# Three low halves of an expert's weights in an earlier turn, and a second-layer block inside three first-layer bodies

## The chip, the cores and the metric

The kernel runs on one core of one Trainium2 chip. The metric is the device time of one execution in microseconds. TensorE is PE below, VectorE is DVE, ScalarE is ACT, GpSimd is POOL, SyncE is SP.

## The reference

Attention over 8 batches and 8 heads, with keys and values averaged over 8 neighbours, gives 4608 tokens of 512 numbers. Tokens with a positive skip score go to one of 8 experts, the others stay as they are.

```python
x = attention(q, mean8(k), mean8(v))            # 4608 x 512
do_compute = x @ w_skip > 0
e_idx = argmax(x[do_compute] @ w_gate, axis=1)  # one expert of 8 per token
for e in range(8):                              # D = 512, F = 1024
    h = np.maximum(xc[e_idx == e] @ w1[e], 0.0)
    y[e_idx == e] = gate_w * (h @ w2[e])
out[do_compute] = xc + y
```

## The kernel before

**Attention and routing.** The attention runs in 36 turns, one for each tile of 128 tokens (`for t in range(NT)`, line 856). While it runs, finished tiles are routed in six groups (`GROUPS`, line 47): for every token of a group its place in a table, ordered by expert, is worked out, and POOL writes the tile's 128 rows into that table in DRAM by an indirect DMA (`write`, line 409; 33 of them). The order on every engine is the order in which the program is written. What POOL does beside its fixed work is handed to a small planner, `gps`, when the program is built: each piece has a first turn, a last turn and a cost, table writes stand in a list of their own, and in every turn `Paced.take` (line 667) puts out pieces of both lists until the turn's budget (`GPS`) is spent or no piece is ready.

**The early expert.** During attention the expert that leads the count so far is chosen, and its weights are loaded in eight chunks of 128 x 1024 (w1 in chunks 0 to 3, w2 in 4 to 7). Products run in fp32r; each weight is split into a high half, a rounded copy by ACT (`high`, line 602), and a low half, the weight less the high one (`low`, line 605), 512 columns at a time. Low halves up to chunk 6, half 0 go to POOL; `later_low` (line 696) gives them to the planner with the turns

```python
gps.add((now["t"] + 1, NT - 6, NT - 6, NT - 1, NT - 1)[max(cc - 2, 0)], wload(cc + 3) - 1 if cc < 3 else (NT - 3, NT - 1, NT + 9, NT + 9)[cc - 3],
        1.25, lambda: low(cc, i))
```

so that chunk 3 and 4 may go from turn 30 on and chunk 5 and 6 from turn 35 on (NT is 36). In the same stretch of POOL's queue stand: the copy of the last batch's values (`values_in`, line 250), read by PE when it makes the values of tile 31; the slots of 256 early tokens and two gathers of their rows (lines 515 and 517), which need ids that an SP transfer reads from the table (line 512); and the writes of the last 15 tiles that are written.

**Slots.** After the last turn, `slots` (from line 1006) works out, for every unit of work, which rows of the table it takes: a chain of some thirty small DVE operations from line 1020 to line 1061 (`coli`) and 1065 (`col`, s_col in the trace). PE needs s_col at line 1068. POOL then gathers the table's rows (line 1062), which needs `coli` and all table writes. A second chain, to line 1102 (s_both), gives the units' kinds, for which PE waits at line 1105; PE reads the gathered rows only at line 1114, behind that. Between these PE works off the first products of the early expert (`steps`).

**The expert loop.** From line 1147 on every engine has a program of its own with semaphores (`P` waits, `V` signals, line 1153). Tokens are worked on in units of up to three blocks ("places") of 128. For each unit PE runs the first layer (`first`, line 1366: 8 groups of 12 products) for a number of columns that depends on the unit's kind: `far_width` (line 1216) holds four bodies, for 256, 320, 288 and 384 columns, and branches to one of them; at its end a body branches to the common code behind all of them (line 1233). There a unit of a kind above TWO runs `second` for place 0 and for place 1 (24 products each), any other unit for place 1 at most; then come the transposes of the next unit and place 2. Within `second(0, True)` the products of k = 4 and k = 6 wait for the last three low halves of the first layer, which DVE writes. The branch hints (`marks`, `branch_hint`) tell the sequencer where a branch leads.

Of the kernel before, what the change touches and what calls it, by code (L numbers as in the profile page):

```python
# [40 lines left out]
NT = NTOK // 128  # L41
# [8 lines left out]
PICK, EARLY = 9, 18  # L50
PICKED = 15
LAST = 6
SCALE = 1.0 / (POOL * HD ** 0.5)
GMAX = max(GROUPS)
PLACED = GROUPS[-1]
# [102 lines left out]
def attention(tc, nc, q, k, vm, vr, cf, wg, w1, w2, whi, wlo, out, c, pay, offs, table, near, bufs, late, early, mb, fin, cfs):  # L158
    with ExitStack() as ctx:
# [38 lines left out]
        def keys(b, hh, gs=slice(0, 4)):  # L198

            r = halves[hh]  # L200
            nc.scalar.activation(kbd[b % 2][r, gs, hh * SP:(hh + 1) * SP], kps[b][r, gs], AF.Copy, scale=-SCALE)

# [116 lines left out]
        def values(t, pT, apart=False):  # L319
            if apart:  # L320
                os = [ps_s.tile([128, 512], F32, name="sc") for _ in range(2)]
            else:
                o = ps_o.tile([128, 2, 512], F32, name="o")
                os = [o[:, 0], o[:, 1]]
            for g in range(4):
                for hh, r, sl, b in blocks(t):
                    nc.tensor.matmul(os[hh][sl, g * VA:(g + 1) * VA], pT[r, g, sl], vb[b % 2][r, g, :], start=(g == 0), stop=False)
            for hh, r, sl, b in blocks(t):
                nc.tensor.matmul(os[hh][sl, 0:4 * VA], pT[r, 4, sl], vl4[b % 3][r].rearrange("p g c -> p (g c)"), start=False, stop=True)
            return [o_.unsqueeze(1) for o_ in os] if apart else [o]  # L330
# [193 lines left out]
        later, now = {}, {}  # L524
# [70 lines left out]
        def load_first(cc):  # L595
            nc.sync.dma_start(chunk_view(stage[:, room(cc)], cc), chunk_src(w1, w2, expert(0), cc))
# [4 lines left out]
        def high(cc, i):  # L601
            nc.scalar.activation(piece(whi, cc, i), stage[:, room(cc), i * 512:i * 512 + 512], AF.Copy)

        def low(cc, i, by=nc.gpsimd):
            return by.tensor_tensor(piece(wlo, cc, i), stage[:, room(cc), i * 512:i * 512 + 512],
                                    piece(whi, cc, i).bitcast(F32), ALU.subtract)
# [82 lines left out]
        act, dve, gps = Work(ACT), Work(DVE), Paced(GPS)  # L689

        def at(t, f):
            loads.setdefault(t, []).append(f)
# [3 lines left out]
        def later_low(cc, i):  # L696
            if cc * 2 + i > 12:
                rest.append(lambda v: low(cc, i, v))
            else:
                gps.add((now["t"] + 1, NT - 6, NT - 6, NT - 1, NT - 1)[max(cc - 2, 0)], wload(cc + 3) - 1 if cc < 3 else (NT - 3, NT - 1, NT + 9, NT + 9)[cc - 3],  # L700
                        1.25, lambda: low(cc, i))

        def adds(b, ready, last):
            first, small = sums(b)
            if b == 0:
                return first, small
            fs = [first[0], first[1], small[0], first[2], small[1], first[3], small[2], small[3]]
            for f, cost in zip(fs, (1.25, 1.25, 0.7, 1.25, 0.45, 0.7, 0.3, 0.7)):
                gps.add(ready, last, cost, f)

        def wload(cc):
            return PICKED + 9 * cc // 4 if cc < 8 else NT - 2
# [17 lines left out]
        for cc in range(8):  # L730
            at(wload(cc), lambda cc=cc: load_first(cc))
            for i in range(2 if cc < LAST else 0):
                act.add(wload(cc) + (3 if cc < 3 else 4), min(wload(cc) + 6, NT - 2), 0.55, lambda cc=cc, i=i: (high(cc, i), later_low(cc, i)))
# [42 lines left out]
        first, small = adds(0, 0, 0)  # L776
# [149 lines left out]
        os_[NT - 1] = values(NT - 1, pts.pop(NT - 1), True)  # L926
        for cc in range(LAST, 8):
            for i in range(2):
                high(cc, i)
                later_low(cc, i)  # L930
# [208 lines left out]
def experts(tc, nc, out, w1, w2, whi, wlo, slot, gate, nti, kinds_a, steps, lows, near, bufs, mb, ident, twice, psum, upper):  # L1139
# [7 lines left out]
    with tc.tile_critical(no_gpsimd_drain=True):  # L1147
# [4 lines left out]
        def P(e, n, by=1):  # L1152
            e.wait_ge(sem[n], by).then_inc(sem[n], -by)  # L1153
# [59 lines left out]
            with when(e, kind > TWO):  # L1213
                three(0, len(QUARTERS) - 1)

        def far_width(e, kind, go, marks):

            name = f"wide{nc.next_id()}"
            widths = [slice(128, 384)] + [slice(0, n) for n in QUARTERS]
            jumps, froms = [], []  # L1220
            for i, n in enumerate(FAR):
                froms.append(nc.cur_bb)
                jumps.append(e.br_cond(kind == TWO + n if n == NEAR else kind < TWO + n + 1, f"{name}_go{i}", f"{name}_not{i}"))
                jumps[i].branch_hint(marks[i])
                nc.switch_bb(f"{name}_not{i}")
            mark = e.mark_branch_hint_location()
            go(widths[-1])
            e.br(f"{name}_past").branch_hint(mark)
            for i, n in enumerate(FAR):
                with nc.body(f"{name}_go{i}", parent=froms[i], valid_engines=[e.engine]):  # L1230
                    mark = e.mark_branch_hint_location()
                    go(widths[n])
                    back = e.br(f"{name}_past")
                    if i + 1 < len(FAR):
                        back.branch_hint(mark)
            nc.switch_bb(f"{name}_past", parent=froms[0])
            return jumps
# [9 lines left out]
        with nc.Block(no_gpsimd_drain=True) as blk:  # L1247
# [89 lines left out]
            def _(t):  # L1337
                at, turn = parity(t, 1)
                
                def tx(u):  # L1340

                    o, after = at(), held[3]
                    t.reg_load(after, nti[0:1, bass.ds(u + 1, 1)])
                    three = t.snap(after, min_val=0, max_val=TWO + 4)
                    if LOOPED:
                        for jump, mark in zip(jumps, widths_ahead(t, after)):
                            jump.branch_hint(mark)
                    for i in range(3):
                        P(t, f"land{i}")
                    for unit, this in ((0, o < 1), (1, o > 0)):  # L1350
                        def place(i, n):
                            for k in range(4):
                                m = t.transpose(psD[i][:, k * 128:k * 128 + 128],
                                                ring[:, 3 * unit + i, k * 128:k * 128 + 128], ident)
                            m.then_inc(sem["pe"], n)

                        with t.If(this):
                            with t.If(three > TWO):
                                place(0, 1)
                                place(1, 1)  # L1360
                            with t.If(three < TWO + 1):
                                place(1, 2)
                            place(2, 1)
                    turn()
# [21 lines left out]
                def second(place, lo):  # L1386

                    i = place % 2
                    if place < 2:
                        P(t, f"psf{i}")  # L1390
                    sl, ps = slice(place * 128, place * 128 + 128), psF[i]
                    for k in range(8):
                        if lo and k in (4, 6):
                            for _ in range(k // 2 - 1):
                                P(t, "lo")
                        t.matmul(ps, hhi[:, k, sl], whi[1][:, k, :], start=(k == 0), stop=False)  # L1396
                        t.matmul(ps, hhi[:, k, sl], wlo[1][:, k, :], start=False, stop=False)  # L1397
                        last = t.matmul(ps, hlo[:, k, sl], whi[1][:, k, :], start=False, stop=(k == 7))  # L1398
                    last.then_inc(sem["l2"], 1)

                def unit(u, kind, ends, _, left):
                    jumps[:] = far_width(t, kind, first, marks)
                    with t.If(kind > TWO):
                        second(0, True)
                        second(1, False)
                    with t.If(kind < TWO + 1):
                        with t.If(kind > TWO - 1):
                            second(1, True)
                    with t.If(left > 1):
                        tx(u)  # L1410
                    with t.If(kind < TWO):
                        for _ in range(3):
                            P(t, "lo")
                    P(t, "psf0")
                    with t.If(ends < 2):
                        second(2, False)
                    with t.If(ends > 1):
                        second_short()
# [40 lines left out]
                marks, jumps = [], []  # L1459
                for n, (_, _, f) in enumerate(steps):  # L1460
                    if n == 5:
                        P(t, "lo")
                    i = int(not 4 <= n < 6)
# [4 lines left out]
                    if n == 3:  # L1468
                        marks = widths_ahead(t, held[1])
                    if n in BETWEEN:  # L1470
                        i = PLACES[BETWEEN.index(n)]
# [248 lines left out]
```

## Time and profile before

| | us |
|---|---|
| median of 3 runs (lowest to highest) | 488.16 (487.16 to 488.66) |
| the profiled execution, its own time | 485.97 |
| its span, first to last instruction | 484.2 |
| busy: PE / DVE / ACT / POOL | 460.1 / 286.7 / 233.8 / 204.2 |

The profile shows one execution. A timeline gives for each instruction its start and its length in us, and in brackets how long its engine was idle before it and which instruction ended that by the semaphores; where an engine waited for several things, the last one is named. "PEq" is PE's sequencer, which runs ahead of the array. Attention ends at about 140 us, the slot calculation runs from 144 to 162 us, the loop over experts from 163 to 479 us, with 11 whole units and one short one.

### The profile page before, as it was taken

Reading aid. Unit: us, or ns where it says so; the run is one execution under the profiler, and the core shown is the slowest. Engines: PE = TensorE matmul, PEld = TensorE weight load, DVE = VectorE, ACT = ScalarE, POOL = GpSimd, SP = SyncE. Lnnn points to the kernel's source line nnn. Section 1 sums busy time; section 2 is a strip of 40 time slices with the busy share of each in tenths; the row PEclk is TensorE's granted clock in tenths of the full one; section 3 lists DMA queues with packets and bytes.
Section 4 is the critical chain, followed back from the end, with each engine's and each line's share of the span. In section 5 each row is a group of like instructions: output and inputs, shape, how many; then the busy total and the mean of one; then the engine's idle time right before and its main releaser. Section 6 shows DMA issues by size and latency. Waiting matters only on the chain. (4 is left out here: it accounts for less than half of the span.)

```text
span 484.2 us, 12494 instructions
## 1 busy us (share of the span) xinstructions
PE 460.1 (95%) x4244; PEld 399.9 (83%) x4245; DVE 286.7 (59%) x659; ACT 233.8 (48%) x614; POOL 204.2 (42%) x271
## 2 busy tenths in 40 slices
PE   8999899999997998999999999999999999999993
PEld 7776677776886787898989899999898989899872
DVE  3677898988879435375765745323226442535663
ACT  4788799999861024173634534221215421424350
POOL 4588279987787331242304034232333222032020
PEclk9999999999998999999999999999999999999998
DMA  8999799966620283657572636111114542234110
GB/s 291 401 405 397 284 364 416 394 219 219 217 73 5 60 283 111 236 200 260 173 238 97 230 129 226 43 43 43 41 51 162 195 162 64 89 128 145 65 43 9
DMA packets 33214, 87.29 MB, mean 180 GB/s; under 512 B 6751, under 2 KB 7263, under 8 KB 31249
## 3 DMA queue, kind: packets, MB, share of 16 engines
q1 hardware_dynamic: 25728, 71.74, 41.0%
q0 software_dynamic: 7440, 14.99, 9.4%
q8 instruction: 24, 0.39, 0.4%
q14 instruction: 22, 0.17, 0.1%
HBM read 72.58 MB, written 20.19 MB: 192 GB/s over the span
## 5 line engine op out<-in xcount | busy, mean ns | idle before, releaser
L1374 PE MATMUL psl<-xhi,w1hi 128*128 128x256 f32 (+3 forms) x352 | 103.5, 294 | 0.3 <-PEq L1153 0.3
L1375 PE MATMUL psl<-xlo,w1hi 128*128 128x256 f32 (+3 forms) x352 | 103.4, 294 | 0.0
L1376 PE MATMUL psl<-xhi,w1lo 128*128 128x256 f32 (+3 forms) x352 | 103.4, 294 | 0.0
L1280 POOL DMA_INDIRECT out<-ring,slot x34 | 35.3, 1038 | 158.6 <-POOLq L1153 144.4
L1500 ACT ACTIVATE hhi<-psl 128x256 fp32r<-128x256 f32 (+3 forms) x88 | 36.2, 411 | 110.5 <-ACTq L1153 109.8
L1573 DVE SCALAR_TENSOR_TENSOR hlo<-psl,hhi 128x256 fp32r<-128x256 f32 (+1 forms) x88 | 38.0, 434 | 59.1 <-DVEq L1153 59.1
L300 ACT ACTIVATE e<-sc,mn 128x72 f32<-128x72 f32 x288 | 64.8, 341 | 9.1 <-DVE mn L295 8.8
L1374 PEld LDWEIGHTS psl<-xhi,w1hi 128*128 128x128 f32 x352 | 66.1, 188 | 1.1 <-issue 0.7
L1375 PEld LDWEIGHTS psl<-xlo,w1hi 128*128 128x128 f32 x352 | 66.1, 188 | 0.4
L1376 PEld LDWEIGHTS psl<-xhi,w1lo 128*128 128x128 f32 x352 | 66.1, 188 | 0.0
L1490 ACT ACTIVATE xhi<-psd 128x512 fp32r<-128x512 f32 x36 | 19.1, 599 | 75.9 <-ACTq L1153 75.9
L1275 POOL DMA_INDIRECT ring<-out,slot x36 | 40.4, 1122 | 19.5 <-issue 15.2
L409 POOL DMA_INDIRECT table<-pay,r_di x33 | 33.1, 1002 | 19.4 <-DVE p_two L434 9.1
L1396 PE MATMUL psf<-w2hi,hhi 128*128 128x512 f32 x96 | 38.2, 398 | 1.8 <-PEq L1153 1.8
L1550 DVE TENSOR_TENSOR w2lo<-stage,w2hi 128x1024 fp32r<-128x1024 f32 x28 | 34.2, 1224 | 9.5 <-DVEq L1153 9.5
L1397 PE MATMUL psf<-w2lo,hhi 128*128 128x512 f32 x96 | 37.5, 390 | 0.0
L1398 PE MATMUL psf<-w2hi,hlo 128*128 128x512 f32 x96 | 37.4, 390 | 0.0
L295 DVE TENSOR_REDUCE mn<-sc 128x4 f32<-128x288 f32 x72 | 30.7, 452 | 11.0 <-PE sc L287 7.2
L1550 DVE TENSOR_TENSOR w1lo<-stage,w1hi 128x1024 fp32r<-128x1024 f32 x28 | 32.4, 1220 | 3.4 <-DVEq L1153 3.3
L1397 PE MATMUL mb<-w2lo,hhi 128*128 128x512 f32 x88 | 34.3, 390 | 0.0
L1396 PE MATMUL mb<-w2hi,hhi 128*128 128x512 f32 x88 | 34.3, 390 | 0.0
L1398 PE MATMUL mb<-w2hi,hlo 128*128 128x512 f32 x88 | 34.3, 390 | 0.0
(293 smaller groups left out, 943.9 us busy)
## 6 DMA issues: line engine op xcount, KB each, us to landing
stage<-in_w SPq DMA_DIRECT2D x64, 512.0 KB, 4.7
out<-x SPq DMA_DIRECT2D x36, 256.0 KB, 5.8
stage<-in_k SPq DMA_DIRECT2D x7, 1152.0 KB, 9.0
qt<-in_q SPq DMA_DIRECT2D x9, 512.0 KB, 7.6
hlo<-in_vm SPq DMA_DIRECT2D x4, 1024.0 KB, 10.4
hhi<-in_vm SPq DMA_DIRECT2D x4, 1024.0 KB, 9.9
xhi<-in_q SPq DMA_DIRECT2D x4, 512.0 KB
xlo<-in_q SPq DMA_DIRECT2D x4, 512.0 KB, 9.6
```

What stands on the lines that cost most here:

```text
L300: nc.scalar.activation(e[:, g, hh * SP:(hh + 1) * SP], sc[:, h * SP:(h + 1) * SP], AF.Exp, bias=mn[:, 4 * i + h:4 * i + h + 1], scale=-1.0)
L1275: g.indirect_dma_start(ring[:, s % 6, 0:D], None, out, bass.IndirectOffsetOnAxis(ap=slot[:, s:s + 1], axis=0), bounds_check=NTOK - 1, oob_ ...
L1280: g.indirect_dma_start(out, bass.IndirectOffsetOnAxis(ap=offsets, axis=0), ring[:, s % 6, 0:D], None, bounds_check=NTOK - 1, oob_is_err=Fa ...
L1374: t.matmul(ps, whi[0][:, k, w], xhi[:, k, xs], start=(k == 0), stop=False)
L1375: t.matmul(ps, whi[0][:, k, w], xlo[:, k, xs], start=False, stop=False)
L1376: last = t.matmul(ps, wlo[0][:, k, w], xhi[:, k, xs], start=False, stop=(k == 3))
L1396: t.matmul(ps, hhi[:, k, sl], whi[1][:, k, :], start=(k == 0), stop=False)
L1397: t.matmul(ps, hhi[:, k, sl], wlo[1][:, k, :], start=False, stop=False)
L1398: last = t.matmul(ps, hlo[:, k, sl], whi[1][:, k, :], start=False, stop=(k == 7))
L1500: a.activation(hhi[:, f, xs], psL[f % 3][:, xs], AF.Relu).then_inc(sem["act"], 1)
L1550: v.tensor_tensor(chunk_of(wlo, c), chunk_view(stage[c], c), chunk_of(whi, c).bitcast(F32), ALU.subtract).then_inc(sem["wlo"], 1)
L1573: return v.scalar_tensor_tensor(out[:, f, :], psL[f % 3][:, xs], 0.0, hhi[:, f, xs].bitcast(F32), ALU.max, ALU.subtract)
```

## The change

A table `LOWS` gives the turns (first, last) of the low halves from chunk 3 on one by one. The two halves of chunk 3 and the first of chunk 4 get turn 29; the second of chunk 4 gets 31 to 33, those of chunk 5 get 32 to 34 and 33 to 35; the first of chunk 6 stays at 35 to 45. Lows of chunks 0 to 2 keep their turns.

`far_width` takes one more argument, code to be put behind a body; it is `second(0, True)`, and it is put into the three bodies that serve kinds above TWO (320, 288 and 384 columns), ahead of the branch to the common code, from which it is taken out.

```diff
+LOWS = (29, 29), (29, 29), (29, 29), (31, 33), (32, 34), (33, 35), (35, 45)
...
-                gps.add((now["t"] + 1, NT - 6, NT - 6, NT - 1, NT - 1)[max(cc - 2, 0)], ...
+                ready, last = LOWS[cc * 2 + i - 6] if cc > 2 else (now["t"] + 1, wload(cc + 3) - 1)
+                gps.add(ready, last,
                         1.25, lambda: low(cc, i))
...
-        def far_width(e, kind, go, marks):
+        def far_width(e, kind, go, marks, then=None):
...
             go(widths[-1])
+            if then:
+                then()
             e.br(f"{name}_past").branch_hint(mark)
...
                     go(widths[n])
+                    if then and n:
+                        then()
                     back = e.br(f"{name}_past")
...
-                    jumps[:] = far_width(t, kind, first, marks)
+                    jumps[:] = far_width(t, kind, first, marks, lambda: second(0, True))
                     with t.If(kind > TWO):
-                        second(0, True)
                         second(1, False)
```

The orders on DVE, ACT and SP are the same in both kernels. In the rows below a name like w1lo<-stage,w1hi is what is written and what is read, and an x2 at the end counts equal instructions in a row. The lines of the changed kernel are 1 to 6 higher than those of the kernel before.

POOL, turn 29 and the start of turn 30, before (w1lo and w2lo are low halves, table<-pay,r_di are table writes, vb is the copy of the last batch's values, nslot and ring the early tokens):

```order
L234 TENSOR_TENSOR vl_124<-ls,cfs 128x4x64
L409 DMA table<-pay,r_di 36864x8
L250 COPY vb_122<-vs 128x4x64
L409 DMA table<-pay,r_di 36864x8
L515 TENSOR_SCALAR nslot<-nids,less 128x2
L517 DMA ring<-out,nslot 128x512 x2
L818 MEMSET stage 81x128x2
L605 TENSOR_TENSOR w1lo<-stage,w1hi 128x512
```

and after:

```order
L235 TENSOR_TENSOR vl_124<-ls,cfs 128x4x64
L606 TENSOR_TENSOR w1lo<-stage,w1hi 128x512 x2
L606 TENSOR_TENSOR w2lo<-stage,w2hi 128x512
L516 TENSOR_SCALAR nslot<-nids,less 128x2
L518 DMA ring<-out,nslot 128x512 x2
L251 COPY vb_122<-vs 128x4x64
L820 MEMSET stage 81x128x2
L410 DMA table<-pay,r_di 36864x8 x2
```

Three lows stand ahead now, the two early gathers come before the copy, and both table writes are behind them.

POOL, the end of its work on the table, before (stage<-table is the gather of line 1062):

```order
L605 TENSOR_TENSOR w2lo<-stage,w2hi 128x512
L409 DMA table<-pay,r_di 36864x8 x2
L605 TENSOR_TENSOR w2lo<-stage,w2hi 128x512
L409 DMA table<-pay,r_di 36864x8 x2
L605 TENSOR_TENSOR w2lo<-stage,w2hi 128x512
L409 DMA table<-pay,r_di 36864x8 x2
L605 TENSOR_TENSOR w2lo<-stage,w2hi 128x512
L409 DMA table<-pay,r_di 36864x8 x2
L1062 DMA stage<-table,s_coli 81x1024
```

and after:

```order
L606 TENSOR_TENSOR w2lo<-stage,w2hi 128x512
L410 DMA table<-pay,r_di 36864x8 x7
L606 TENSOR_TENSOR w2lo<-stage,w2hi 128x512
L410 DMA table<-pay,r_di 36864x8 x2
L1064 DMA stage<-table,s_coli 81x1024
```

Behind the first low shown, one low stands among nine writes, where three stood among eight.

PE, the end of the body of 320 columns, before, in the order of the code (psl is the first layer's product, the rows behind the branch belong to the next body):

```order
L1374 MATMUL psl_3122<-xhi,w1hi 128x320
L1375 MATMUL psl_3122<-xlo,w1hi 128x320
L1376 MATMUL psl_3122<-xhi,w1lo 128x320
L1233 UNCONDITIONAL_BRANCH
L1223 COMPARE_AND_BRANCH
L1374 MATMUL psl_3121<-xhi,w1hi 128x288
```

and the start of the common code, before (psf is place 0, the first row is the branch of the last body):

```order
L1228 UNCONDITIONAL_BRANCH
L1403 COMPARE_AND_BRANCH
L1396 MATMUL psf_3127<-w2hi,hhi 128x512
L1397 MATMUL psf_3127<-w2lo,hhi 128x512
L1398 MATMUL psf_3127<-w2hi,hlo 128x512
```

The end of the body of 320 columns after:

```order
L1380 MATMUL psl_3122<-xhi,w1hi 128x320
L1381 MATMUL psl_3122<-xlo,w1hi 128x320
L1382 MATMUL psl_3122<-xhi,w1lo 128x320
L1402 MATMUL psf_3127<-w2hi,hhi 128x512
L1403 MATMUL psf_3127<-w2lo,hhi 128x512
L1404 MATMUL psf_3127<-w2hi,hlo 128x512
```

and its last rows with the branch:

```order
L1402 MATMUL psf_3127<-w2hi,hhi 128x512
L1403 MATMUL psf_3127<-w2lo,hhi 128x512
L1404 MATMUL psf_3127<-w2hi,hlo 128x512
L1239 UNCONDITIONAL_BRANCH
L1225 COMPARE_AND_BRANCH
```

Place 0 follows the first layer without a branch between, and the branch comes behind it.

## Rows read from the trace of the kernel before

**Rows 1.** page, section 1: busy us, share of the span, instructions

```profile
PE 460.1 (95%) x4244; PEld 399.9 (83%) x4245; DVE 286.7 (59%) x659; ACT 233.8 (48%) x614; POOL 204.2 (42%) x271
```

**Rows 2.** stretches: length, busy us of PE, PEld, DVE, ACT, POOL, clock, DMA

```profile
149.30:152.40 3.10, 0.00 (x0) 0.00 (x1) 3.00 (x14) 0.00 (x0) 2.62 (x4) 1.00 0.01 1
152.40:157.00 4.60, 4.57 (x19) 3.97 (x20) 4.40 (x15) 0.60 (x1) 2.40 (x3) 0.63 0.04 6
...
172.40:186.70 14.30, 14.29 (x96) 14.04 (x96) 4.47 (x15) 3.06 (x7) 4.32 (x6) 1.00 0.77 272
186.70:188.50 1.80, 0.00 (x0) 0.03 (x1) 0.56 (x2) 1.34 (x2) 0.00 (x0) 1.00 0.02 5
188.50:468.00 279.50, 279.50 (x1692) 253.76 (x1692) 141.36 (x222) 103.66 (x172) 75.16 (x93) 1.00 0.40 134
```

**Rows 3.** PE timeline: start, length, operation [idle before it, what ended it]

```profile
152.43 0.42 PE L1068 MATMUL sc<-cfs,s_col 81*128 81x81 f32 x2 [3.17 <-DVE s_col L1065]
...
158.89 0.30 PE L1105 MATMUL sc<-cfs,s_both 81*1 81x81 f32 x2
```

**Rows 4.** timeline of DVE, the slot calculation

```profile
144.16 0.16 DVE L404 TENSOR_SCALAR r_di<-mb 128x3 int32<-128x3 f32 x1 [0.19 <-issue]
...
145.14 1.95 DVE L1026 TENSOR_TENSOR s_ni<-s_n,nskip 128x8 int32<-128x8 f32 x1
...
148.82 2.02 DVE L1044 TENSOR_SCALAR s_le<-s_end,cfs 128x8 f32<-128x8 f32 x1
...
152.13 0.15 DVE L1065 TENSOR_TENSOR s_col<-s_col 128x1 f32<-128x1 f32 x1
...
158.18 0.16 DVE L1102 TENSOR_REDUCE s_both<-s_kind 128x1 f32<-128x8 f32 x1
```

**Rows 5.** timeline of POOL from turn 29 to the last table write

```profile
122.23 1.01 POOL L409 DMA_INDIRECT table<-pay,r_di  x1 [3.98 <-DVE l L347]
123.24 0.41 POOL L250 COPY vb<-vs 128x256 f32<-128x256 f32 x1
...
124.86 0.30 POOL L515 TENSOR_SCALAR nslot<-nids,less 128x2 int32<-128x2 f32 x1
...
127.87 0.35 POOL L818 MEMSET stage<- 81x256 f32 x1
...
145.74 1.31 POOL L605 TENSOR_TENSOR w2lo<-stage,w2hi 128x512 fp32r<-128x512 f32 x1
...
149.51 1.28 POOL L605 TENSOR_TENSOR w2lo<-stage,w2hi 128x512 fp32r<-128x512 f32 x1
...
152.27 0.98 POOL L409 DMA_INDIRECT table<-pay,r_di  x1 [0.31 <-issue]
```

**Rows 6.** timeline of PE, end of the first unit's first layer

```profile
186.39 0.30 PE L1376 MATMUL psl<-xhi,w1lo 128*128 128x320 f32 x1
188.50 0.47 PE L1396 MATMUL psf<-w2hi,hhi 128*128 128x512 f32 x1 [1.81 <-PEq L1153]
188.81 0.40 PE L1397 MATMUL psf<-w2lo,hhi 128*128 128x512 f32 x1
189.04 0.40 PE L1398 MATMUL psf<-w2hi,hlo 128*128 128x512 f32 x1
```

**Rows 7.** branch of line 1233: ns min/median/max, first and last start

```profile
L1233 PEldq COMPARE_BRANCH  x10: 179/179/4264, 183.9 to 412.7; - x10
```

**Rows 8.** high halves of ScalarE, line 602, same columns

```profile
L602 ACT ACTIVATE w2hi<-stage x8: 618/622/628, 108.1 to 138.2; 128x512 fp32r<-128x512 f32 x8
```

**Rows 9.** timeline of PE, the values of tile 31

```profile
125.82 0.41 PE L327 MATMUL o<-vb,pT 64*64 64x74 f32 x9
```

**Rows 10.** gather of line 1062, same columns, and its time to landing

```profile
L1062 POOL DMA_INDIRECT stage<-table,s_coli x1: 1076/1076/1076, 155.4 to 155.4; - x1
...
DMA to landing us min/median/max: 4.1/4.1/4.1
```

**Rows 11.** line 348, the normalised tile on DVE

```profile
L348 DVE TENSOR_TENSOR x<-o,rc x35: 674/679/681, 20.6 to 138.2; 128x512 f32<-128x512 f32 x35
```

More of the change, by code (lines that the diff above doesn't have):

```diff
@@ L699, in later_low @@
             else:
-                gps.add((now["t"] + 1, NT - 6, NT - 6, NT - 1, NT - 1)[max(cc - 2, 0)], wload(cc + 3) - 1 if cc < 3 else (NT - 3, NT - 1, NT + 9, NT + 9)[cc - 3],
+                ready, last = LOWS[cc * 2 + i - 6] if cc > 2 else (now["t"] + 1, wload(cc + 3) - 1)
+                gps.add(ready, last,
                         1.25, lambda: low(cc, i))
```

## The prediction

> **What bounds the kernel now.** I read the busy shares first, then a table of stretches, then the idle places of TensorE (PE) in time, then what the waited-for engine did. PE is busy for 95% of the span [rows 1]. The table shows where the rest goes [rows 2]: the loop over experts, 188.5 to 468 us, is PE without a hole (279.50 of 279.50 us), so a time gained or lost before it moves the end one for one. Ahead of it stand two holes: 149.3 to 152.4 us with no product at all, and 186.7 to 188.5 us, again with none.
>
> The first hole: PE waits 3.17 us for s_col, which VectorE (DVE) writes at line 1065 [rows 3]. DVE is not idle there. Its slot calculation runs from 144.16 to 152.28 us, all of it tiny operations of 0.15 to 0.2 us, but two of them took 1.95 and 2.02 us [rows 4]. Each ends within 0.05 us of the end of a low half on GpSimd (POOL): 147.09 against 145.74 + 1.31 = 147.05, and 150.84 against 149.51 + 1.28 = 150.79 [rows 4, 5]. So the low half holds them. Measured against a normal operation (0.16) that is 1.79 + 1.86 = 3.65 us on the chain for which PE waits. Right behind the hole the granted clock is 0.63 over 4.6 us, so PE loses another 4.6 x 0.37 = 1.7 us there; behind the 1.8 us hole it is 1.00 [rows 2]. PE does not pay all of that: at 158.89 its next product needs s_both, ready at 158.34 [rows 3, 4], so with PE faster DVE would be the bound 0.4 us sooner (0.55 less the 0.15 from 152.28 to 152.43 that a hand-over takes).
>
> The second hole: the first product of the second layer starts 2.11 us after the last one of the first, where 0.15 us is the spacing (14.3 us for 96): 1.96 us lost [rows 2, 6]. The branch that ends a first-layer body (line 1233) shows why: ten of them, nine of about 0.18 us, and one, the first, at 183.9 us, of 4.26 us [rows 7]. The sequencer took it 2.6 us ahead of the end of the body (186.54), which hid that much: 4.26 less 2.6, and 0.3 us from its end to the product, gives 1.96. It is a cost of the first pass through that code.
>
> **The change, part by part.** Lows: POOL runs the same 7 lows and 15 table writes from 118.25 us on, in another order. Before, it is idle for 3.98 us at 118.25 [rows 5]. Now three lows stand there, 3 x 1.28 = 3.84 us. Their inputs are there: the youngest is the first w2 high half, ScalarE at 108.1 us [rows 8]. So nothing that follows is later by them alone, and everything that did not wait comes earlier. What is moved behind them: nslot and the two early gathers (3.01 us by 124.86 to 127.87) run at 122.1 instead of 124.9. The copy of the last batch's values (line 250) went at 123.24 and now goes at 122.1 + 3.0 = 125.1, done at 125.5; PE reads it at 125.82 [rows 5, 9]: 0.3 us of cover, so I cost it at nothing; without it, each us late is a us on the turns. The two table writes come after that, without a waiter before line 1062. The ids that nslot reads come from the table by a transfer that must be over before the write at 122.23 may change it: they were in by then.
>
> The tail of POOL is what counts. Write by write (1.30), low by low (1.28 plus 0.17 to the next write), it ends its last write at about 149.8 us instead of 153.25, and only one low, the last, falls into 144 to 152: at about 146.1 to 147.4. DVE's chain should be held once instead of twice: half of 3.65 = 1.8 us gained. Bounds: 0, if the seven writes in a row hold DVE as much, and 3.65, if the low misses the chain. I take the middle since a chain of 4 to 6 us that starts at 144.16 can hardly miss it. s_both then comes at 156.5 and PE goes on at 156.7 instead of 158.89. PE itself is there by 155.4, if its hole is now 1.4 us and its clock stays at 1.00 as behind the 1.8 us one, or by 157.1 if not. Gain 2.2 us; 1.8 if the clock falls again. The gather at line 1062 started 2.1 us after the last write ended (155.4 against 153.25) and landed after 4.1 us [rows 5, 10]: now 151.9 and 156.0, ahead of the 156.7 of PE, which needs it after s_both only. Hidden, with 0.7 us to spare.
>
> The Trainium skill, page "SBUF — State Buffer", section "Who interferes with whom", says that a VectorE instruction with two SBUF inputs and a GpSimd one that reads SBUF share a port, which the first one keeps for its whole instruction. By that a hold is worth no more than the low, 1.3 us, and the sum would be 0.5 us smaller; the rows show holds of 1.8 us, so the measurement stands.
>
> Place 0: the 24 products and their waits are not changed in number; they stand in three bodies (320, 288, 384 columns) ahead of the branch instead of behind it. In all later units that is nothing: their branch takes 0.18 us, and PE has no hole there [rows 2, 7]. In the first unit the branch is not gone, it comes 24 products later and leads to code that is still unread. I take it to cost 4.26 us again. What it has now as cover is the same lead, 2.6 / 0.149 = 17.5 products, but of the second layer, 0.23 us each [rows 6]: 4.0 us. Left over: 4.26 + 0.3 - 4.0 = 0.55 us, a gain of 1.96 - 0.55 = 1.4 us. Bounds: 1.96, if the code has arrived by then, and 0, if the lead is cut, since the products of k = 6 wait for the last low half of the first layer. POOL, ScalarE and SyncE issue the same in the loop.
>
> On that branch the Trainium skill, page "Runtime: NRT & Kernel Launch", section "Instruction fetch mechanics", has a rule that speaks against the change: a taken branch to code outside the window stalls until it is fetched. By it the wait is moved, not removed, and the sum would keep only what the longer cover hides; the 4.26 us of the first pass agree.
>
> **Sum.** 2.2 + 1.4 = 3.6 us. The profiled execution took 485.97 us (span 484.2), so 482.4; the median of the runs shown is 488.16, 2.2 above it, and I hold the prediction against that: 488.16 - 3.6 = 484.6 us.
>
> **The rivals.** (a) The last low misses the chain or meets an operation that it does not hold: 3.65 + 0.4 + 1.4 = 5.45, 482.7 us. For it: only two operations of the chain were held, so others pass. Against: each of the two lows in it caught one. (b) The branch costs PE its 1.96 us again, behind place 0, by a lead that is cut short: 2.2 alone, 486.0 us. (c) The chain stalls as before, since table writes stand in for lows: 1.4 alone, 486.8 us, no measurable change. For it: both holds began 0.6 to 0.7 us ahead of the low, beside the write before it [rows 4, 5]. Against: both ended with the low, and no operation was held like that without one. (d) Slower: the three lows, now in the middle of turn 29, hold operations of DVE there as the last two did in the slot chain, 3 x 1.8 = 5.4 us on the turns, if DVE has no slack in them; 5.4 - 3.6 = 1.8 us slower, 490.0 us. It decides from 3.6 + 1.5 = 5.1 us on. Against it: in 35 tiles the operation of line 348 never took more than 681 ns beside 674 at least [rows 11], though lows and sums ran on POOL all through the turns.
>
> **How the numbers follow.** The forecast has a chance of 0.55, with a range of its own of 483.7 to 485.5; (a) 0.10, (b) 0.13, (c) 0.15, (d) 0.07. A measurement of this kernel tells about 0.3% (1.5 us) from no change. Faster by more: 0.54 + 0.10 + 0.11 + 0.04 = 0.79. Within: 0.01 + 0.02 + 0.11 + 0.01 = 0.15. Slower: 0.06. The range: 3.65 + 0.4 + 1.96 = 6.0 us of gain at the one end, 482.2, and at the other a little less than (c), 1.0 us, 487.2. Only (d) is left out.
>
> **What would show it.** Right: POOL without its 4 us idle at 118 us; one DVE operation near 2 us between 144 and 152 us, not two; s_col near 150.5; clock 1.00 after it; the expert loop's first product near 2.2 us earlier; the branch ahead of the common code once near 4.3 us, and a hole of some 0.5 us behind place 0 of the first unit. Wrong: two long DVE operations still there, the values of tile 31 late on PE, or a hole of 2 us that has only moved to place 1.

## The result and the profile after

The changed kernel took 492.03 us (median of 7 runs, 491.33 to 494.65), the kernel before 488.16 beside it: 1.0093 times, with an interval of 1.0066 to 1.0121. It is 0.9% slower, and 4.8 us above the upper end of the range.

The profiled execution is one of 492.03 us, its span 490.2 us. Busy time by engine is within 4 us of what it was [rows 1]:

```profile
PE 463.5 (95%) x4244; PEld 401.6 (82%) x4245; DVE 282.8 (58%) x659; ACT 234.4 (48%) x614; POOL 203.9 (42%) x271
```

A table of stretches (length; busy time of PE, PEld, DVE, ACT, POOL; clock; DMA), cut by the same events in each kernel: from DVE's line 343 or 344 of the 29th turn to the end of attention, from there to the first product of the expert loop, and the loop to the last product. First the kernel before (the trace of rows 1 to 11):

```profile
118.20:139.10 20.90, 20.40 (x398) 16.14 (x397) 17.56 (x66) 19.30 (x66) 14.97 (x17) 1.00 0.47 156
139.10:163.00 23.90, 19.71 (x134) 17.68 (x132) 18.62 (x81) 4.09 (x7) 15.12 (x16) 0.93 0.10 29
163.00:475.90 312.90, 309.78 (x1866) 279.71 (x1866) 155.34 (x250) 113.02 (x187) 85.34 (x104) 1.00 0.40 136
```

and the changed kernel:

```profile
119.10:152.70 33.60, 26.58 (x401) 19.68 (x402) 17.80 (x65) 21.25 (x67) 24.98 (x26) 0.90 0.32 105
152.70:170.96 18.26, 17.24 (x128) 15.71 (x126) 14.12 (x81) 2.48 (x5) 2.88 (x4) 1.00 0.08 22
170.96:481.90 310.94, 309.62 (x1866) 279.79 (x1866) 155.41 (x250) 112.95 (x187) 85.25 (x104) 1.00 0.41 137
```

The two stretches for which a gain was forecast are shorter, by 5.6 and 2.0 us. The last turns of attention, which were to stay as they were, take 12.7 us longer. One turn, the 34th, holds half of it. Before, it takes 4.19 us between the reciprocals that DVE makes of o, and eight products of line 329 take 0.68 us:

```profile
130.70 0.21 DVE L343 RECIPROCAL rc<-o 128x8 f32<-128x8 f32 x1
134.89 0.20 DVE L343 RECIPROCAL rc<-o 128x8 f32<-128x8 f32 x1
133.79 0.68 PE L329 MATMUL o<-vl,pT 64*64 64x296 f32 x8
```

PE in that turn of the changed kernel (start, length, operation, in brackets the idle time before it):

```profile
138.78 2.08 PE L330 MATMUL o<-vl,pT 64*64 64x296 f32 x7
141.15 0.41 PE L330 MATMUL o<-vl,pT 64*64 64x296 f32 x1 [0.29 <-issue]
141.86 0.54 PE L543 MATMUL sc<-cfs,ring 128*128 128x128 f32 x3 [0.31 <-issue]
...
143.30 0.49 PE L312 MATMUL pt<-cfs,e 128*128 128x128 f32 x3 [0.46 <-issue]
144.73 0.37 PE L312 MATMUL pt<-cfs,e 128*128 128x128 f32 x1 [0.94 <-issue]
```

and DVE, which is to read the o that line 330 ends at 141.56:

```profile
139.78 0.17 DVE L383 TENSOR_TENSOR r_oh<-mb,r_c 128x16 bf16<-128x16 f32 x1
146.34 0.21 DVE L344 RECIPROCAL rc<-o 128x8 f32<-128x8 f32 x1 [6.39 <-PE pt L313]
```

PE waits for nothing that the profile shows ("issue"), and yet its instructions come singly or in small groups, many of them in steps of some 0.72 us; the eight products of line 330, 0.68 us before, take 2.78. And what it has finished is not known to DVE for 4.8 us. The same happens, smaller, at 122 to 124.4 us. The clock does not explain it: it is granted in full there and falls only behind it, to 0.50, the lower of its two levels (1.2 GHz of 2.4), from 144.1 to 150.9 us; nor are the DMA engines busy (a share of 0.05):

```profile
138.20:144.00 5.80, 4.26 (x48) 2.07 (x47) 1.58 (x8) 2.19 (x10) 4.28 (x6) 1.00 0.05 8
144.10:150.90 6.80, 4.75 (x83) 4.03 (x87) 3.67 (x15) 4.50 (x8) 3.00 (x3) 0.50 0.12 42
```

POOL in that time:

```profile
134.65 1.29 POOL L606 TENSOR_TENSOR w2lo<-stage,w2hi 128x512 fp32r<-128x512 f32 x1
136.10 0.99 POOL L410 DMA_INDIRECT table<-pay,r_di  x1 [0.16 <-issue]
...
143.86 0.98 POOL L410 DMA_INDIRECT table<-pay,r_di  x1 [0.30 <-issue]
148.20 1.27 POOL L606 TENSOR_TENSOR w2lo<-stage,w2hi 128x512 fp32r<-128x512 f32 x1 [3.36 <-ACT w2hi L603]
```

The row of seven table writes ends at 144.84, and PE's signals come from 146.32 us on, five within 0.3 us. Of some 200 signals of PE to other engines in the attention part, 17 are missing in the record of this trace. Matched in their order, some 20 of the others are recorded over 0.35 us behind the end of their product, up to 4.8 us, each of them while or just after POOL issues an indirect DMA. In the trace of the kernel before not one is. Which signals are missing is not known, so the 20 is a rough count; that DVE and ScalarE start late is not.

### The profile page after: what moved, and what is told of

Read it like the earlier page. It is cut to its first block, busy times and chain, and to the rows that moved or that the text cites. A ratio compares the mean times of both kernels' runs of the same rounds, so it can differ in the third digit from the quotient of the medians.

```text
span 490.2 us, 12493 instructions
## 1 busy us (share of the span) xinstructions
PE 463.5 (95%) x4244; PEld 401.6 (82%) x4245; DVE 282.8 (58%) x659; ACT 234.4 (48%) x614; POOL 203.9 (42%) x271
## 2 busy tenths in 40 slices
DMA packets 33216, 87.34 MB, mean 178 GB/s; under 512 B 6750, under 2 KB 7262, under 8 KB 31248
## 5 line engine op out<-in xcount | busy, mean ns | idle before, releaser
L1286 POOL DMA_INDIRECT out<-ring,slot x34 | 36.4, 1072 | 153.1 <-POOLq L1155 140.9
L1281 POOL DMA_INDIRECT ring<-out,slot x36 | 39.4, 1094 | 20.9 <-issue 16.7
```

The lines of the kernel that those rows point to most:

```text
L1281: g.indirect_dma_start(ring[:, s % 6, 0:D], None, out, bass.IndirectOffsetOnAxis(ap=slot[:, s:s + 1], axis=0), bounds_check=NTOK - 1, oob_ ...
L1286: g.indirect_dma_start(out, bass.IndirectOffsetOnAxis(ap=offsets, axis=0), ring[:, s % 6, 0:D], None, bounds_check=NTOK - 1, oob_is_err=Fa ...
```

## The experiments

The theories at the start: **S**, PE is held back while POOL issues table writes in a row, and the change made a row of seven; **B**, the three lows in turn 29 cost it; **C**, the two parts only do harm together; **R** (later **L**), it belongs to that execution. Each run gave a ratio to the kernel before on the same chip.

| run | chip's time for the kernel before | ratio (95%) |
|---|---|---|
| the changed kernel, first | 488.2 | 1.0093 (1.0066 to 1.0121) |
| e1_lows | 484.2 | 0.9934 (0.9908 to 0.996) |
| e2_place0 | 484.2 | 0.9987 (0.9953 to 1.0021) |
| e3_front | 484.2 | 0.994 (0.991 to 0.9971) |
| e4_tail | 484.2 | 1.004 (1.0008 to 1.0072) |
| e5_after | 483.9 | 0.9914 (0.9888 to 0.994) |
| e6_front_place0 | 483.9 | 0.9938 (0.9905 to 0.9972) |
| e7_late_low | 483.8 | 0.9905 (0.9869 to 0.9942) |
| e8_after | 483.8 | 0.9964 (0.9938 to 0.9989) |
| e9_spaced | 489.6 | 1.0073 (1.0039 to 1.0107) |
| e10_after | 489.6 | 1.014 (1.0036 to 1.0244) |
| e11_gaps | 488.6 | 1.0091 (1.006 to 1.0122) |
| e12_before | 488.6 | 1.000 (0.997 to 1.0031) |
| e13_long | 483.5 | 0.9978 (0.9941 to 1.0016) |
| e14_pairs_late | 483.5 | 0.9986 (0.9951 to 1.0022) |
| e15_place0 | 483.5 | 0.9995 (0.9963 to 1.0027) |
| e16_long | 487.7 | 0.9979 (0.9946 to 1.0012) |

There are two kinds of chips here, told apart by the kernel before itself: 484 us (four chips, called A: e1 to e4, e5 and e6, e7 and e8, e13 to e15) and 488 to 490 us (three chips, called B: e9 and e10, e11 and e12, e16; the first measurement is like them). Each chip was used for one set of runs only, so whether the kind belongs to the chip or to the time is not shown; A and B stand for either.

**One part alone, and the order of the lows.** e1 takes place 0 back into the common code; e2 gives the lows the turns of before; e3 and e4 change the table:

```diff
e1 -jumps[:] = far_width(t, kind, first, marks, lambda: second(0, True))
   +jumps[:] = far_width(t, kind, first, marks)      # second(0, True) under t.If again
e2 +LOWS = (30, 33), (30, 33), (30, 35), (30, 35), (35, 45), (35, 45), (35, 45)
e3 +LOWS = (29, 29), (29, 29), (29, 29), (30, 35), (35, 45), (35, 45), (35, 45)   # and e1
e4 +LOWS = (30, 33), (30, 33), (30, 33), (31, 33), (32, 34), (33, 35), (35, 45)   # and e1
```

> The lows' part alone; the loop is that of the kernel before. In the trace of the changed kernel PE executes some instructions from 138.9 to 146.2 us at a spacing of 0.72 us, and its semaphores reach DVE and ACT up to 5 us late (once more at 122 to 124.4). Theory S (while POOL issues seven table writes in a row, PE is held back): the same stall at the same place, so about 492.0 + 1.9 = 494 us, 1.012 times the kernel before. Rival R (the stall belongs to that one execution, not to the order): a trace without the stall, and a time near 488 - 2 = 486 us.

> Place 0 in three bodies alone; POOL's order is that of the kernel before. The hole of 1.8 us at 186.7 us in the first unit goes: 488.2 - 1.8 = 486.4 us, 0.996 times the kernel before (the forecast gave 1.4 of these). If the branch behind place 0 costs PE as much as the one it replaces: 488.2 us, 1.000.

> Lows' part in another form, loop as before: the same three lows in turn 29, the other four where the kernel before has them in turns, which puts seven table writes in a row some 8 us earlier than in the changed kernel (from turn 30 on), and four in a row later. Theory S: PE held back beside those seven writes, 5 us or more lost, about 493 us. Rival B (the three lows in turn 29 alone are what costs, by what they hold up on DVE and by the late copy of the values): the loss is that of the turns up to 130 us, some 3 us, and none beside the writes.

> No low in turn 29 (POOL as in the kernel before up to turn 31), but three lows in a row and then six table writes in a row from some 140 us on, loop as before. Theory S: PE held back beside the six writes, by some 5 us: 493 us. Rival B: no stall, one hold in the slot calculation instead of two, 488.2 - 1.8 = 486.4 us.

No stall in any of them, though e1 and e3 have seven writes in a row and e4 six. Theory S in its plain form fell, and so did B: on this chip, of kind A, the three lows in turn 29 are free, since e1 takes 20.9 us from the 29th turn to the end of attention, to 0.1 us what the kernel before takes. e1 gained as forecast. e4 missed both expectations: its slot calculation is 2.8 us shorter than that of before, but PE has holes of 1.53, 1.44 and 1.95 us ("issue") at 43, 51 and 103 us, where its program is that of the kernel before. Such holes at 43 and 51 us are in the trace of before too (0.40 and 1.44) and not in those of e3 and e5. So e4 has 4.9 us of them against 1.8, which takes back the 2.8. What brings them is open.

**The changed kernel again, on other chips.**

> The changed kernel once more, beside other runs of the kernel before. Alone, the lows' part gave 0.9934 and place 0 gave 0.9987, without any stall of PE at 122 to 146 us. Theory L (the stall is one of how the instructions of PE arrive in certain executions, not of the order on POOL): about 0.9934 + 0.9987 - 1 = 0.992 times the kernel before, 480.3 us beside 484.2, and a trace without PE instructions at a spacing of 0.72 us. Rival C (the two parts together bring it about): 1.009 again, 488.5 us beside 484.2, with the stall at the same place, some 139 to 146 us.

> Both parts, with the lows in the other order (three in turn 29, the rest in the turns of the kernel before, as in the run with that order alone, which gave 0.994). Theory L: 0.994 + 0.9987 - 1 = 0.993, 480.7 us beside 484.2. Rival C: slower than the kernel before, by 4 us or more, with PE held back in the last turns.

0.9914 and 0.9938: C fell. In the trace of e5 the stretches are:

```profile
116.10:137.00 20.90, 20.40 (x397) 16.12 (x396) 17.56 (x65) 19.30 (x66) 18.39 (x20) 1.00 0.47 156
137.00:158.03 21.03, 18.20 (x133) 16.43 (x132) 16.23 (x82) 4.11 (x7) 11.45 (x13) 1.00 0.11 33
158.03:469.10 311.07, 309.63 (x1865) 279.66 (x1866) 155.24 (x250) 113.04 (x187) 86.74 (x104) 1.00 0.41 137
```

The last turns are equal to before to 0.1 us, the slot calculation is 2.9 us shorter, the loop 1.8. So the forecast's mechanism is there, on this chip. PE, DVE and the branch of line 1239 in the same trace:

```profile
148.32 0.42 PE L1070 MATMUL sc<-cfs,s_col 81*128 81x81 f32 x2 [1.15 <-DVE s_col L1067]
...
153.82 0.44 PE L1107 MATMUL sc<-cfs,s_both 81*1 81x81 f32 x4 [0.54 <-DVE s_both L1104]
```

```profile
143.25 1.89 DVE L1030 TENSOR_SCALAR s_half<-s_ni 128x8 int32<-128x8 int32 x1
```

```profile
L1239 PEldq COMPARE_BRANCH  x10: 179/182/412, 183.0 to 410.2; - x10
```

One operation held instead of two [rows 4], 1.15 us of hole instead of 3.17 [rows 3], a clock of 1.00 behind it instead of 0.63 [rows 2], and a branch that never takes more than 0.41 us [rows 7]. Place 0 follows the first layer of the first unit without a hole, where 1.81 us stood [rows 6]:

```profile
181.20 0.31 PE L1382 MATMUL psl<-xhi,w1lo 128*128 128x320 f32 x1
181.35 0.39 PE L1402 MATMUL psf<-w2hi,hhi 128*128 128x512 f32 x1
```

**The held operation, and what the chip is.** e7 hands the last low of POOL out behind the gather:

```diff
+            elif cc * 2 + i == 12:
+                behind.append(lambda: low(cc, i))
...
             if wait == "":
+                behind.pop()()
```

> The changed kernel with the last low half of POOL (chunk 6, half 0) moved out of the slot calculation, behind the gather that follows the last table write; nine writes now stand in a row. Theory H (a low half in the slot calculation holds one DVE operation for its length, and PE waits for that): in the trace of the changed kernel on a chip without the stall the one hold is 1.89 us, PE's hole ahead of s_col 1.15 us and that ahead of s_both 0.54 us; both go, so 1.7 us less than the changed kernel: 0.988 times the kernel before. If table writes hold DVE as lows do: 0.991, with a long operation still there. Theory S' (while POOL issues table writes, PE's signals come late, but only in sessions of the kind of the first measurement): in such a session (the kernel before at 488 us and not 484) this kernel is slower than the changed one, by 1 to 3 us, since nine writes stand in a row instead of seven.

> The changed kernel beside it. Two sessions have given opposite results for it: 492.0 us beside 488.2 (1.0093), and 479.6 beside 483.9 (0.9914). In the trace of the first, 33 signals of PE came 0.5 to 4.8 us late, each while POOL issued an indirect DMA; in that of the second none did. Theory S': if the kernel before takes 484 us here, 0.991 and no late signals; if it takes 488 us, about 1.009, with PE late beside the row of seven writes.

An A chip. No DVE operation before s_col is held any more and PE's hole there is gone, though a row of nine table writes runs beside the chain to 146.0 us:

```profile
146.67 0.34 PE L1073 MATMUL sc<-cfs,s_col 81*128 81x81 f32 x2
```

Lows hold DVE, writes do not. The hole before s_both grew from 0.54 to 1.05 us, with the low now beside the second chain, so of the 1.7 us some 0.9 arrived and the forecast of 0.988 was missed: 20.0 us from the end of attention to the loop, against 20.9 in e8. The changed kernel's ratio of 0.9964 here and 0.9914 on the other A chip shows the scatter.

**On B chips.** e9 spreads the writes:

```diff
+LOWS = (29, 29), (29, 29), (29, 29), (31, 33), (33, 35), (36, 45), (36, 45)
```

> Both parts, with the last low halves of POOL later, so that its table writes stand in rows of 2, 5, 3, 3 and 2 between lows and not 2, 2, 2, 7 and 2. Where PE's signals come in time this is the changed kernel's time, 0.991 to 0.996 times the kernel before: the last low lies in the slot calculation in both. Theory S': in a session in which the kernel before takes 488 us, the loss of the changed kernel in the last turns (6.5 us in one turn beside seven writes) is smaller here, about 3 us, 488 us in all.

> The changed kernel beside it, for the session: 0.991 to 0.996 if the kernel before takes 484 us, about 1.009 with late PE signals if it takes 488 us.

This chip was of kind B, and the stall came back. DVE in e10:

```profile
140.18 0.17 DVE L383 TENSOR_TENSOR r_oh<-mb,r_c 128x16 bf16<-128x16 f32 x1
146.76 0.21 DVE L344 RECIPROCAL rc<-o 128x8 f32<-128x8 f32 x1 [6.40 <-PE mb L393]
```

A second trace, and the same 6.4 us at the same place: R fell as well. It is the order, but on B chips only. e9 did no better: it has the loss in two pieces, one beside its row of five writes, one beside a row of three that ends at 149.45 us, though a low stands ahead of that row.

e11 puts pauses into the row of seven, by small memsets after every second write and between the two early gathers:

```diff
+            def apart(self, most):
+                if self.row >= most:
+                    nc.gpsimd.memset(near["gap"], 0.0)     # 128 x 256
+                    self.row = 0
+                self.row += 1
...
```

> The changed kernel with four small memsets on POOL (128 x 256, about 0.35 us each) that keep its indirect DMAs apart: one between the two early gathers, three in the row of seven writes, so that no more than two stand in a row. Theory S' (on some chips PE's signals wait until POOL's row of indirect DMAs is over, and pass in a gap of 0.5 us): on a chip on which the kernel before takes 488 to 490 us, the 6.5 us lost beside the seven writes and the 2.1 us beside the two gathers go, most of them: 0.995 to 1.000 times the kernel before instead of 1.009 to 1.014. On a chip on which it takes 484 us: 0.991 to 0.997, up to 1 us more than the changed kernel for the later end of POOL's writes. Rival (the stall hangs on the lows or on the number of writes, not on rows): 1.01 on a chip of the first kind.

> The kernel before, for a trace of it on this chip. On a chip on which it takes 484 us: no late PE signals, holes of PE as in the first trace. On one on which it takes 488 us or more: late PE signals by 0.5 to 1.5 us beside its writes, which stand alone or in pairs, and some 4 us lost to them.

A B chip, and a miss: 1.0091. In its trace POOL is off its DMAs for 0.5 us at a time, and DVE still waits:

```profile
147.25 0.21 DVE L344 RECIPROCAL rc<-o 128x8 f32<-128x8 f32 x1 [6.12 <-PE mb L393]
```

(That profiled execution took 500.41 us, 7.5 over the median, 4.9 of them by a hole in the loop at 228 us, at the wait told of under place 0.) e12 gives the kernel before on a B chip:

```profile
120.30:146.50 26.20, 23.11 (x400) 17.83 (x400) 18.05 (x67) 21.35 (x67) 22.95 (x23) 1.00 0.32 105
146.50:165.10 18.60, 17.50 (x129) 15.90 (x128) 14.07 (x81) 2.48 (x5) 5.29 (x7) 1.00 0.07 22
165.10:477.20 312.10, 309.73 (x1866) 279.74 (x1866) 155.48 (x250) 113.18 (x187) 86.58 (x104) 1.00 0.40 136
```

Two things are to be seen. Its last turns are 5.3 us longer than on an A chip: PE's signals come late beside its writes too. And its slot calculation takes 18.6 us and not 23.9: PE is so late that POOL has its lows done before the chain begins, and there is no hole left to gain. On a B chip the lows' part can win only 0.3 us (18.6 against 18.26).

The traces show why 0.5 us may be too short. On B chips the signals that are kept back come in a bunch, the first of it 0.5 us behind the end of the second of two early gathers (123.90 us in the first trace), 1.12 us behind a row of five writes (e9, 136.20 us) and 1.48 us behind the row of seven (144.84 us).

The last theory, S'': PE's signals get through only in a pause of about a low's length, as the lows between the pairs of writes of the kernel before give it. e13 and e16 put such pauses into the row of seven, and nothing else (the edit is against e11; its pause between the gathers is gone):

```diff
-                    nc.gpsimd.memset(near["gap"], 0.0)
+                    for _ in range(2):
+                        nc.gpsimd.tensor_tensor(near["gap"], cfs[:, 0:256], cfs[:, 0:256], ALU.add)
```

> The changed kernel with pauses of 1.3 us (two sums of 128 x 256 on POOL, of no use) in the row of seven writes, after every second one. Theory S'' (PE's signals come through only in a pause of about a low half's length): on a chip on which the kernel before takes 488 us, the turn of 10.7 us comes down to some 5 us and the time to 0.995 to 0.999; on one on which it takes 484 us, POOL's writes end 3.9 us later, the gather with them, and most of the gain in the slot calculation is lost: 0.994 to 0.999. Rival (something else in that turn): 10 us again and 1.009.

> The changed kernel with the pauses of 1.3 us, as in e13_long (0.998 on a chip at 483.5 us). If the kernel before takes 488 us here: theory S'' says the turn of 10.7 us comes down to some 5 us, and 0.995 to 0.999; the rival, 10 us and 1.009. If it takes 484 us: 0.998 again, and the question stays.

e13 fell on an A chip, where the later end of the writes brings back a hole of 2.55 us before s_col and leaves 0.9978. e16 fell on a B chip: 0.9979 where the changed kernel without pauses had 1.009 and 1.014. POOL and DVE in its trace:

```profile
137.06 0.99 POOL L410 DMA_INDIRECT table<-pay,r_di  x1 [0.30 <-DVE lg L353]
138.07 1.33 POOL L667 TENSOR_TENSOR ngap<-cfs 128x256 f32<-128x256 f32 x2
139.55 0.99 POOL L410 DMA_INDIRECT table<-pay,r_di  x1 [0.15 <-issue]
```

```profile
135.47 0.21 DVE L344 RECIPROCAL rc<-o 128x8 f32<-128x8 f32 x1 [1.24 <-PE o L330]
139.69 0.20 DVE L344 RECIPROCAL rc<-o 128x8 f32<-128x8 f32 x1
```

The turn that took 10.7 us takes 4.22 (135.47 to 139.69). The changed kernel without pauses was not run on this chip, but the 30th to 32nd turns are those of the other B chips (5.23, 3.42 and 3.77 us against 5.34, 3.40 and 3.81 in the first trace). The lengths of the three turns in question, from the starts of that line (the 30th, 32nd and 34th, each less the one ahead):

| kernel, chip | 30th | 32nd | 34th |
|---|---|---|---|
| before, A / B | 3.21 / 5.01 | 3.46 / 3.77 | 4.19 / 4.51 |
| changed, A (e5) | 3.21 | 3.46 | 4.19 |
| changed, B (first / e10) | 5.34 / 5.31 | 3.81 / 3.79 | 10.69 / 10.70 |
| rows of 5 and 3, B (e9) | 5.32 | 8.04 | 8.71 |
| pauses of 0.5 us, B (e11) | 4.03 | 3.48 | 10.43 |
| pauses of 1.3 us, B (e16) | 5.23 | 3.77 | 4.22 |

**Place 0 and a mixture.** e14 takes e7 with the lows in the turns of before; e15 is e2 again.

> Place 0 in the bodies, POOL's lows in the turns of the kernel before (writes alone or in pairs), but the last low behind the gather, out of the slot calculation; four writes stand in a row at the end, when attention is over. One of the two holds of DVE goes (1.9 us), and the hole of place 0: on a chip at 484 us 0.992 to 0.995; on one at 488 us, where the slot calculation has no such hole, place 0 alone: 0.996 to 1.000, not 1.009.

> Place 0 alone, once more: 0.996 to 0.999 on either kind of chip, since POOL's order is that of the kernel before. If the larger code costs something where PE's instructions come slowly: 1.002 or more on a chip at 488 us.

Both within the scatter. e14 missed by a wait of its own: the last low, behind a gather that is late there, comes 3.8 us after PE asks for it (line 575). e15 and e2 show why place 0 gives less than its hole: PE, now earlier, waits for the gathered rows of a later unit, as here in e2,

```profile
219.49 0.31 PE L1359 MATMUL psd<-cfs,ring 128*128 128x128 f32 x1 [0.59 <-PEq L1155]
```

and by 0.35 to 1.1 us in eight of the twelve other traces with that code, e11 aside.

## Why the prediction was wrong

- **The first hole, lows.** The mechanism was right and is shown by e1, e5 and e7: a low in the slot calculation holds one DVE operation, PE waits for it, and with one low less PE is earlier by 2.9 us on an A chip (2.2 forecast). Of the 0.7 us more, 0.5 is DVE's second part: s_col to s_both went from 6.06 to 5.59 us. The held operation took 1.89 us again, more than the low beside it (1.32), and began 0.54 us ahead of it. By the Trainium skill ("SBUF — State Buffer", section "Who interferes with whom") the engine that comes first keeps the shared port for its whole instruction, by an estimate from that 1.32 us at most here; the measured hold is again longer. On a B chip the term is 0.3 us, since the hole that it was to fill is not there.
- **The step that failed** stands in "The change, part by part": "nothing that follows is later by them alone", and of the writes moved behind them only "without a waiter before line 1062". I priced a write by who waits for its data, and the row of seven writes, which the order showed, at nothing on the turns; of the seven the prediction asked only whether they hold DVE. On B chips it costs 10.7 less 4.5, 6.2 us, in one turn (the last turns as a whole: 33.6 us against 26.2 in e12, with a clock of 0.50 behind the stall). With the 1.9 us of the first hole that are not to be had there, that is 8.1 us, somewhat more than the 7.4 from the forecast to the result. That pauses of 1.3 us after every second write take the 6.2 us away is shown by e16, one run on one chip; that 0.5 us are too short, by e11. e11's pauses were memsets and e16's sums, so that the length alone decides is not shown, and e9 lost as much with a low ahead of its row of three. By what PE's signals are kept back is not shown.
- **The rivals.** (c) was about writes that hold DVE as lows do; e7 shows that they don't. (d) had the sign and nearly the time (490.0), but by lows in turn 29 that hold DVE; those cost nothing on an A chip, and on a B chip that turn is long in the kernel before too (5.01 against 5.34).
- **The second hole, place 0.** 1.4 us was forecast, and the hole of 1.81 us went whole. The branch takes 0.41 us at most, not 4.26 once, so the bound of 1.96 was the nearer value for that trace. But the trace of rows 6 and 7 has the longest hole: in the four others without place 0 in the bodies (e1, e3, e4, e12) the first branch takes 3.52 to 3.93 us and the hole 1.07 to 1.47 us. Part of it is given back at the next unit's rows: the loop is shorter by 1.2 to 1.8 us. Alone it gave 0.9987 and 0.9995, with intervals that hold both no change and the forecast. The Trainium skill's rule of a taken branch that stalls for code outside the window ("Runtime: NRT & Kernel Launch", section "Instruction fetch mechanics") would have moved the wait; this trace shows no such stall behind place 0.
- **The base.** I carried 2.2 us from the profiled execution (485.97) to the median (488.16) as a constant. By their signs they were of two kinds of chip: the profile has no late signal, its records of signals are as many as on A chips (6777), and its slot calculation has the hole that a B chip lacks. The forecast, 0.993 of the kernel before, is what A chips give (0.9914 and 0.9964).

## What to carry to other kernels

An indirect DMA that POOL issues has a price beside that of its data: before several are put in a row, look at what the order of before had between them, for that work may be what lets other engines' signals through. A profile is one execution on one chip: where the median of the runs lies 0.5% off it, price the change for a trace of the other kind too, and ask of each hole whether it is there in both. Two kernels with the change were run on both kinds: the one with pauses (e13, e16) was not slower on either, 0.998 on both, with intervals that hold no change; the changed kernel is the better one on A chips, the kernel before on B chips.

## What the runs showed of the hardware

- On three chips, and in the first measurement, PE's signals came up to 5.6 us late while POOL issued indirect DMAs back to back, and PE's own instructions came in steps of some 0.72 us, at a granted clock of 1.00; on four others, with the same orders of the changed kernel and of the one with pauses, no such thing. Pauses of 0.5 us after every second DMA did not help (10.43 us for the turn), pauses of 1.3 us did (4.22).
- In the traces of the three chips and of the first measurement of the changed kernel a tenth of the records of signals is missing (6021 to 6143, against 6750 to 6784 on the others), which by itself tells the kind.
- Whether the recording of the profile has a part in it stays open.
- On A chips a low half on POOL held one small DVE operation for 1.7 to 2.0 us, longer than itself (1.3); indirect DMAs, nine in a row, held none.
